# Attention and a gated MLP in one kernel: tokens walked from last to first, weights loaded over 128 partitions, and new orders from a changed plan

## The chip, the core and the metric

The kernel runs on one core of one Trainium2 chip. The metric is the device time of one execution in microseconds (us); the time of before is the median of three runs. A profile of one further execution, with its trace, is read for the reasons.

## The reference, cut to what matters

The input is x, 2048 tokens of 448 features, in bfloat16. The first half is attention in 16 heads of 28, in which a token sees 8 tokens at distances 0, 2, ..., 14 before it. The second half is an MLP whose gate mixes all tokens by a 2048x2048 matrix.

```
def _A_ref(x, wqkv, wo):            # W, dil = 8, 2
    q, k, v = (x @ wqkv) in 16 heads of 28
    idx = pos[:, None] - arange(W) * dil      # mask idx < 0
    logits = einsum('bhsd,bhswd->bhsw', q, k[idx]) * scale
    o = einsum('bhsw,bhswd->bhsd', softmax(logits), v[idx])
    return o @ wo
def _B_ref(x, w_in, w_sp, b_sp, w_out):
    z = gelu(x @ w_in)                        # 1792 columns
    z1, z2 = z[..., :896], layernorm(z[..., 896:])
    g = einsum('ts,bsf->btf', w_sp, z2) + b_sp[None, :, None]
    return (z1 * g) @ w_out
h = x + _A_ref(layernorm(x), A_wqkv, A_wo)
h2 = h + _B_ref(layernorm(h), B_w_in, B_w_sp, B_b_sp, B_w_out)
```

## The kernel before, in words

**Layout.** The 2048 tokens are 16 blocks of 128; block u and block u+8 make unit u (8 units), since the two halves of the sequence are worked on side by side. The 448 features are 7 chunks (NC7) of 64, so that two matmuls with 64 rows each run beside each other on TensorE: the first half of the tokens on partitions 0 to 63, the second half on 64 to 127 (index s in the loops). So each weight has to stand twice, on both halves of the partitions. Before, it is loaded from memory to partitions 0 to 63 (`ld_w` L546, `ld_win` L556, seven rows of 64 partitions), and VectorE (DVE) or ScalarE (ACT) copies it to the other half (`t_cp` L748, `cpw` L569). For q and k the copies also spread the heads from 28 to 32 columns. The weights of q and k are staged in z2p; those of v go straight to reg1 (reg1, reg2 and reg3 are memory that holds different things one after the other).

**The stages.** `ln_unit` (L633) normalizes a unit: statistics of two blocks on DVE (L639, L640), the reciprocal root on GpSimd (L629, L630) or ACT (L651, L652), the normalization on DVE into a ring tile tring (L659), and a transpose into xh, either on TensorE (L675, with a copy out of PSUM, L624 or L626) or by a transposing DMA (L666). For the first layernorm, `DMA_T` says which units go by DMA: 3 to 7. Then come the products for q and k (L787, in four column ranges CQ and CK of 128, 128 or 142, 256 and 512 tokens), nine attention tiles of 114 tokens (values L825, logits L859, exp L871, band mask L878, sums L887, weighted values L907, ln and exp for the division L895 and L917, the division L925), the output product L960 with the residual L968, the second layernorm, z2 (L980) and z1 (L1024), the big token mixing (L1060), its gate (L1069, L1077), and the last product (L1089), whose eviction with the residual (L1099) goes to tring and from there to memory (L1104). Names in the plan: x7 is the load of block 7, mmq3_0 a q product of column range 3, mmv8 the values of tile 8, tD1_4 the transposing DMA of unit 4 in the first layernorm, wsp0_8 and wsp1_8 the transposing loads of block 8 of the mixing matrix (two halves), bb the bias load.

**The halo.** The second half of the sequence begins at token 1024 and needs the 14 tokens ahead of it. Before, these are loaded again (xhalo, L576), normalized apart (L693 to L718: statistics, root, L700, seven small transposes L708, a copy L715) and put into the columns ahead of xh; the k product then runs over 1038 columns instead of 1024.

**What sets the order.** `Sched.issue` (L99) records instructions with their semaphore waits. `SEQ` (L34) holds for each of five queues (SP, POOL, DVE, ACT, PE) the tasks in the order in which they are issued; `Planner.replay` (L289) walks these lists with modelled durations, and its result decides only which PSUM banks and ring slots a task takes. An engine works off its list in order: a task that waits holds up all behind it. Loads are issued by SP and ACT (SPq and ACTq in the trace). Loads of blocks of units 2 to 7 wait until block 8 has landed (L585).

**Fillers.** f0 (15 matmuls on a constant tile, L618), f1 and f2 (3 each) keep TensorE busy while the first units are normalized.

Of the kernel before, what the change touches and what calls it, by code (L numbers as in the profile page):

```python
# [6 lines left out]
D = 448  # L7
DH = 28
FH = 896
# [14 lines left out]
DMA_T = {1: range(3, 8), 2: range(8)}  # L24
# [196 lines left out]
class Planner:  # L221
# [21 lines left out]
    CHUNK, ASK, NEED = 256, 118, 434  # L243
    FETCH = (0.95, 2.5)

    def fetch(self, nmm, now, dur, commit=False):

        n, m = self.pe_n, 2 * nmm
        ka, kn, free, av, shift = self.k_ask, self.k_need, self.f_free, self.avail, 0.0
        new = []  # L250
        while True:
            a, b = self.CHUNK * ka + self.ASK, self.CHUNK * kn + self.NEED
            if min(a, b) > n + m:
                break
            if a < b:
# [33 lines left out]
    def replay(self, t0=0.7):  # L289
# [13 lines left out]
        for _ in tasks:  # L303
# [26 lines left out]
            if e == "pe":  # L330
                if t.nmm:
                    dur += self.fetch(t.nmm, now, dur, True)
# [830 lines left out]
```

## Time and profile before

| | |
|---|---|
| median of 3 runs | 248.61 us (247.55 to 248.67) |
| the profiled execution | 246.46 us, of which the span is 244.4 us |
| PE (TensorE) busy | 234.2 us, 96% of the span |
| DVE, ACT, GpSimd busy | 142.3, 88.8, 26.9 us |

The span is the time from the first to the last instruction that the profiler saw; 2.06 us of the profiled execution lie around it. Rows of the timeline give start, duration, engine, line, operation, the tiles written and read, the shape and the count, and in brackets how long the engine had stood idle before and what ended that. "issue" there means that nothing the profile shows was waited for. PEld is the loading of weights into TensorE, which overlaps the matmuls.

### The profile page before, as it was taken

How to read it: one execution, taken by the hardware profiler on the slowest of the kernel's cores; microseconds unless marked ns; L12 is line 12 of the kernel's file. 1: busy time of each engine (PE TensorE's matmuls, PEld its weight loads, DVE VectorE, ACT ScalarE, POOL GpSimd, SP SyncE). 2: the span in 40 equal slices, each digit the busy share in tenths (PEclk: the TensorE clock that was granted, in tenths of full speed). 3: DMA queues.
4: the chain of work that ended last, by engine and by line, in shares of the span. 5: the costliest groups of instructions: out<-in, count | busy, mean ns of one | idle time of the engine just before them, and what ended most of it. 6: DMA issues, size and time to landing. Idle time of an engine off the chain costs nothing.

```text
span 244.4 us, 6704 instructions
## 1 busy us (share of the span) xinstructions
PE 234.2 (96%) x3021; PEld 120.7 (49%) x3032; DVE 142.3 (58%) x283; ACT 88.8 (36%) x104; POOL 26.9 (11%) x67
## 2 busy tenths in 40 slices
PE   6878998999999999999999999999999999999995
PEld 2675863455555454544444444444444444444443
DVE  7995984969999799887900013244011417541844
ACT  2886967188978857765730000000000000000000
POOL 5051300000330050137200000000000000000000
PEclk9999999999999999999999999999999999999999
DMA  6964394793669955665545443200000000010113
GB/s 149 276 117 96 75 134 74 100 159 70 89 69 120 165 160 103 107 133 105 118 91 155 88 86 86 46 0 0 0 0 3 0 0 0 21 38 18 56 58 113
DMA packets 54580, 20.02 MB, mean 82 GB/s; under 512 B 46856, under 2 KB 54424, under 8 KB 54552
## 3 DMA queue, kind: packets, MB, share of 16 engines
q1 hardware_dynamic: 52728, 18.05, 38.7%
q10 hardware_dynamic: 1824, 1.55, 3.1%
q8 instruction: 23, 0.38, 0.7%
q14 instruction: 5, 0.04, 0.1%
HBM read 6.39 MB, written 1.84 MB: 34 GB/s over the span
## 4 chain that ended last, share of the span: by engine, by line
PE 83%; DMA 9%; DVE 4%; issue 2%; SPq 1%; ACT 0%; DVEq 0%
PE psum L1060 39%; PE psum L980 9%; PE psum L1024 9%; PE psum L1089 9%; DMA wspT_lo<-in_B_w_sp_dram 6%; PE psum L787 5%; PE psum L960 4%; PE psum L825 4%; PE psum L859 1%; DMA xh<-tring 1%; PE psum L907 1%; DVE st L639 1%; DMA reg<-in_A_wo_dram 1%; PE psum L675 1%; DVE tring L659 1%
## 5 line engine op out<-in xcount | busy, mean ns | idle before, releaser
L1069 DVE TENSOR_TENSOR ub<-psum,reg 128x512 bf16<-128x512 f32 x28 | 18.8, 687 | 67.4 <-PE psum L1060 67.3
L1060 PE MATMUL psum<-reg,z2p 128*128 128x512 bf16 x219 | 49.4, 379 | 0.3
L1060 PE MATMUL psum<-wspT_lo,z2p 128*128 128x512 bf16 x218 | 48.5, 379 | 0.4 <-issue 0.2
L1060 PEld LDWEIGHTS psum<-wspT_lo,z2p 128*128 128x128 bf16 x224 | 21.8, 98 | 26.6 <-issue 0.4
L1060 PEld LDWEIGHTS psum<-reg,z2p 128*128 128x128 bf16 x224 | 21.9, 98 | 26.1
L787 PE MATMUL psum<-xh,reg 64*128 64x128 bf16 (+3 forms) x448 | 26.1, 270 | 1.2 <-issue 1.1
L980 PE MATMUL psum<-w_in,xh 64*128 64x448 bf16 x224 | 22.4, 349 | 0.1
L1089 PE MATMUL psum<-reg 128*128 128x448 bf16 (+1 forms) x119 | 22.3, 341 | 0.0
L1024 PE MATMUL psum<-xh,w_in 64*128 64x512 bf16 x196 | 22.0, 376 | 0.0
L787 PEld LDWEIGHTS psum<-xh,reg 64*128 64x128 bf16 x448 | 17.1, 94 | 9.0 <-issue 2.1
L624 ACT ACTIVATE reg<-psum 128x896 bf16<-128x896 f32 (+3 forms) x23 | 19.0, 843 | 3.6 <-PE psum L825 2.5
L639 DVE BATCH_NORM_STATS2 st<-x_tm 128x6 f32<-128x448 bf16 x32 | 19.5, 608 | 0.1
L996 DVE BATCH_NORM_STATS2 st<-z2p 128x6 f32<-128x448 bf16 x32 | 17.6, 607 | 2.4 <-ACT z2p L990 2.4
L871 ACT ACTIVATE reg<-psum 128x928 bf16<-128x928 f32 x18 | 16.2, 940 | 5.4 <-PE psum L859 5.4
L1099 DVE TENSOR_TENSOR tring<-psum,x_tm 128x448 bf16<-128x448 f32 (+1 forms) x17 | 9.8, 593 | 14.3 <-PE psum L1089 14.2
L1034 ACT ACTIVATE reg<-psum 128x1024 bf16<-128x1024 f32 x14 | 13.7, 1030 | 9.3 <-PE psum L1024 9.3
L1089 PEld LDWEIGHTS psum<-reg 128*128 128x128 bf16 x119 | 11.6, 98 | 10.2
L990 ACT ACTIVATE z2p<-psum 128x896 bf16<-128x896 f32 x16 | 14.1, 921 | 5.3 <-PE psum L980 5.2
L980 PEld LDWEIGHTS psum<-w_in,xh 64*128 64x128 bf16 x224 | 10.7, 94 | 10.7 <-issue 0.4
L630 POOL TENSOR_TENSOR rs<-rs,nhalf 128x2 f32<-128x2 f32 x20 | 15.5, 777 | 1.7
L1024 PEld LDWEIGHTS psum<-xh,w_in 64*128 64x128 bf16 x196 | 9.5, 94 | 11.4 <-ACT reg L1034 0.2
L629 POOL TENSOR_SCALAR rs<-mv 128x2 f32<-128x2 f32 x20 | 5.3, 263 | 87.7 <-DVE mv L640 77.4
(66 smaller groups left out, 201.7 us busy)
## 6 DMA issues: line engine op xcount, KB each, us to landing
out_dram<-tring SPq DMA_DIRECT2D x15, 112.0 KB, 1.7
x_tm<-in_A_x_dram SPq DMA_DIRECT2D x13, 112.0 KB, 4.6
w_in<-in_B_w_in_dram SPq DMA_DIRECT2D x2, 448.0 KB, 5.4
z2p<-in_A_wqkv_dram ACTq DMA_DIRECT2D x2, 392.0 KB, 6.0
reg<-in_B_w_out_dram SPq DMA_DIRECT2D x1, 784.0 KB, 4.8
w_in<-in_B_w_in_dram SPq DMA_DIRECT2D x2, 336.0 KB, 5.1
reg<-in_B_b_sp_dram SPq DMA_DIRECT2D x1, 512.0 KB, 3.7
reg<-in_A_wo_dram SPq DMA_DIRECT2D x4, 98.0 KB
```

The costliest lines, as they stand in the source:

```text
L624: iss("act", lambda e: e.activation(dst, src, AF.Copy), reads=rd, writes=wr)
L630: iss("pool", lambda e: e.tensor_tensor(dst, dst, nh, ALU.pow), reads=rr + [r_nhalf], writes=rr)
L639: iss("dve", lambda e: e.bn_stats(st[:, b, :], x_tm[:, b, :]), reads=[r_x[b]], writes=[rl[b]])
L787: iss("pe", lambda e, c=c, s=s, gi=gi, lhs=lhs: e.matmul(psum[:, bk[s] * 512 + cw * gi:bk[s] * 512 + cw * gi + cw], lhs, xh[64 * s:64 * s ...
L871: iss("act", lambda e: e.activation(E[:, es[0], 2 * n:2 * n + 2, :], pair_view(lb, 0, 8 * JW), AF.Exp, scale=SCALE), reads=[r_bank[lb[0]], ...
L980: iss("pe", lambda e, c=c, s=s: e.matmul(psum[:, zb[s] * 512:zb[s] * 512 + D], xh[64 * s:64 * s + 64, c, HX + 128 * u:HX + 128 * u + 128], ...
L990: iss("act", lambda e: e.activation(z2p[:, u:u + 9:8, D * k:D * k + D], pair_view(zb, 0, D), AF.Gelu_apprx_tanh), reads=[r_bank[zb[0]], r_ ...
L996: iss("dve", lambda e, b=b: e.bn_stats(st3[:, b, k, :], z2p[:, b, D * k:D * k + D]), reads=[r_z2[b][k]], writes=[r_st3[b][k]])
L1024: iss("pe", lambda e, c=c, s=s: e.matmul(psum[:, bk[s] * 512:bk[s] * 512 + 512], w_in[64 * s:64 * s + 64, c, 128 * f:128 * f + 128], xh[64 ...
L1060: iss("pe", lambda e, b=b: e.matmul(psum[:, gb[0] * 512:gb[0] * 512 + 512], z2p[:, b, 128 * f:128 * f + 128], src[:, b, 512 * (tc % 2):512 ...
L1069: iss("dve", lambda e: e.tensor_tensor(ub[:, us_[0], :], psum[:, gb[0] * 512:gb[0] * 512 + 512], bb[:, 512 * tc:512 * tc + 512], ALU.add), ...
L1089: iss("pe", lambda e, f=f: e.matmul(psum[:, wb[0] * 512 + d0:wb[0] * 512 + d1], z1p[f][:, 128 * m:128 * m + 128], w_out[:, f, d0:d1], star ...
```

## The change

Parts that belong together:

1. Units and attention tiles run from last to first. Unit 7 (blocks 7 and 15) comes first, tile 8 is the first tile; `S_ORDER` runs backward too, so that the mixing starts with blocks 7 and 15.
2. The halo is a copy: the 14 columns are copied on DVE from unit 7's xh on the other half of the partitions (`xpad`) for the values, and in kT (`kh`) for the keys. The load, the statistics and the seven small transposes go; the k product has 1024 columns. An attention tile's queries are shifted by 2 columns, and the mask with them.
3. Weights are loaded as 128-partition pieces: 384 rows as 3 x 128, the last 64 rows apart. Block m of the piece then holds chunk 2m on the lower and chunk 2m+1 on the upper half. Copies go crosswise between the halves (`cross`, and 16 copies instead of 8 for q and k), and `BLK` gives the order in which a half meets its chunks.
4. The plan's model of TensorE's instruction fetch counts a fetch into the queue of the loads (`resolve`); all lists in SEQ are new. The six pieces of wqkv and four x loads may go by SP or by ACT (`both`).
5. In the new lists f1 and f2 stand behind all other work of PE, and five of the last products (blocks 1, 6, 7, 0, 11) behind the split one of block 15.

```diff
-DMA_T = {1: range(3, 8), 2: range(8)}
+DMA_T = {1: range(5), 2: range(8)}
+BLK = ((0, 2, 4, 6, 1, 3, 5), (1, 3, 5, 0, 2, 4, 6))
...
+    def resolve(self, until, n=0):
+
+        while len(self.avail) < len(self.asks):
+            en = max([self.asks[len(self.avail)]] + self.avail[-1:]) + self.FETCH[0]
+            if en > until and len(self.avail) >= n:
+                break
+            st = max(en, self.qfree)
+            self.qfree = st + self.OCC
+            self.avail.append(st + self.FETCH[1])
...
+        def w_view(dst, src):
+            return ((dst[:, 0:3, :], src[0:384].rearrange("(m p) n -> p m n", p=128), 302.0),
+                    (dst[0:64, 3, :], src[384:448], 178.0))
...
-            t_w[p] = dma(eng, "w" + p, lambda e: e.dma_start(
-                w_st[p], A_wqkv[:, c0:c0 + D].rearrange("(c p) n -> p c n", p=64)),
-                D * D * 2, writes=[r_st[p]], bw=172.0)
+            for n, (dst, src, bw) in enumerate(w_view(w_st[p], A_wqkv[:, c0:c0 + D])):
+                t_w[p].append(dma(eng, "w%s%d" % (p, n), lambda e, dst=dst, src=src: e.dma_start(dst, src),
+                                  (384, 64)[n] * D * 2, writes=[r_st[p][n]], bw=bw, both=True))
+        def cross(name, w, rs, deps, n):
...
+            for h, lo, nb in ((0, 4, 3), (1, 3, 4)):
...
+                    copy(tk[0].eng, w[64 * h:64 * h + 64, lo:NC7, :], w[64 - 64 * h:128 - 64 * h, 0:nb, :], rs[:-2], [rs[h - 2]])
...
-        t_xhalo = dma("sp", "xhalo", lambda e: e.dma_start(xhalo[:, :], X[ST - 16:ST, :]), 16 * D * 2, writes=[r_xhalo])
...
+        t_xpad = cst("xpad", [(lambda e: e.tensor_copy(xh[64:128, :, HX - HALO:HX], xh[0:64, :, HX + ST - HALO:HX + ST]),
+                               [r_xh[NU - 1]], [r_xpad[1]])], 0.2, eng="dve", deps=[t_xh[NU - 1]])
...
-        CQ = [0, 128, 256, 512, ST]
-        CK = [0, 128, 270, 526, ST + HALO]
+        CQ = [0, 512, 768, 896, ST]
+        CK = [HALO + c for c in CQ]
...
+        t_kh = cst("kh", [(lambda e: e.tensor_copy(kT[:, 1, :, 0:HALO], kT[:, 0, :, ST:ST + HALO]), r_k[NCH - 1], [r_kh])], 0.15,
+                   eng="dve", deps=t_k[NCH - 1] + [c_kpad])
...
+        t_cp["v", 0] = cross("cpv", wv, r_w["v"], t_w["v"], D)
...
-        S_ORDER = [b for u in range(NU) for b in (u, u + 8)]
+        S_ORDER = [b for u in range(NU - 1, -1, -1) for b in (u, u + 8)]
...
+            t_hT[u] = ln_unit(u, 2, [th, th], [t_xpad] if u == NU - 1 else [])
```

The beginning of ACT's list, before, where the first loads are issued (x_tm blocks, then the weights of k and q into z2p, later v into reg1):

```order
L541 DMA x_tm<-in_A_x_dram 128x448 x3
L548 DMA z2p<-in_A_wqkv_dram 64x7x448 x2
L498 ACT_TABLE_LOAD
L651 ACTIVATE rs<-mv,epst 128x2
L652 ACTIVATE rs<-rs 128x2
L651 ACTIVATE rs<-mv,epst 128x2
L652 ACTIVATE rs<-rs 128x2
L624 ACTIVATE reg<-z2p 64x7x8x28
L624 ACTIVATE xh<-psum 128x7x128
L624 ACTIVATE reg<-z2p 64x7x8x28
L548 DMA reg<-in_A_wqkv_dram 64x7x448
```

The same stretch of ACT's list in the changed kernel (block 7, then q in two pieces, the small piece of v, the big piece of k):

```order
L539 DMA x_tm<-in_A_x_dram 128x448
L552 DMA z2p<-in_A_wqkv_dram 128x3x448
L552 DMA z2p<-in_A_wqkv_dram 64x448
L552 DMA reg<-in_A_wqkv_dram 64x448
L552 DMA z2p<-in_A_wqkv_dram 128x3x448
L494 ACT_TABLE_LOAD
L654 ACTIVATE rs<-mv,epst 128x2
L655 ACTIVATE rs<-rs 128x2
L627 ACTIVATE reg<-z2p 64x3x8x28
L654 ACTIVATE rs<-mv,epst 128x2
L655 ACTIVATE rs<-rs 128x2
L627 ACTIVATE reg<-z2p 64x4x8x28
```

Two of the three x loads have left ACT's queue, q stands ahead of k, and a piece of every weight is issued ahead of the table load. The other pieces are in SP's list, which begins with x14, x15, x6, the big piece of v, x13, x9, x12, the small piece of k, x4, x2 and two pieces of w_in.

The beginning of PE's list, before, and then in the changed kernel:

```order
L618 MATMUL psum<-warm 128x512 x15
L675 MATMUL psum<-ident,tring 128x128 x7
L618 MATMUL psum<-warm 128x512 x3
L675 MATMUL psum<-ident,tring 128x128 x7
L618 MATMUL psum<-warm 128x512 x3
L708 MATMUL psum<-ident,thalo 128x16 x7
L787 MATMUL psum<-xh,reg 128x142 x56
L787 MATMUL psum<-xh,reg 128x128 x168
L859 MATMUL psum<-reg 64x58 x64
L825 MATMUL psum<-reg,xh 64x448 x56
```

```order
L621 MATMUL psum<-warm 128x512 x15
L678 MATMUL psum<-ident,tring 128x128 x14
L769 MATMUL psum<-xh,reg 128x128 x28
L809 MATMUL psum<-reg,xh 64x448 x56
L769 MATMUL psum<-xh,reg 128x128 x196
L678 MATMUL psum<-ident,tring 128x128 x7
L844 MATMUL psum<-reg 64x58 x96
L769 MATMUL psum<-xh,reg 128x256 x112
```

The fillers between the transposes and the halo's transposes are gone, the first product of q is followed by the values of tiles 8 and 7, and all 224 matmuls of the first two column ranges have 128 columns.

The end of PE's list, before, and then in the changed kernel:

```order
L1060 MATMUL psum<-reg,z2p 128x512 x16
L1089 MATMUL psum<-reg 128x448 x14
L1060 MATMUL psum<-reg,z2p 128x512 x16
L1089 MATMUL psum<-reg 128x448 x21
L1089 MATMUL psum<-reg 128x224 x14
```

```order
L1050 MATMUL psum<-reg,z2p 128x512 x16
L1079 MATMUL psum<-reg 128x448 x21
L1079 MATMUL psum<-reg 128x224 x14
L1079 MATMUL psum<-reg 128x448 x35
L621 MATMUL psum<-warm 128x512 x6
```

Five products of full width now follow the two of half width, and the six filler matmuls come last.

More of the change, by code (lines that the diff above doesn't have):

```diff
@@ L243, with fetch @@
     CHUNK, ASK, NEED = 256, 118, 434
[L244 to L250, printed above, removed]
+    FETCH, OCC, DMA_LAT = (1.09, 2.55), 0.72, 1.15
+    def resolve(self, until, n=0):
[6 more added lines that the diff above has]
+            self.avail.append(st + self.FETCH[1])
+    def fetch(self, nmm, now, dur):
+        n, m, shift = self.pe_n, 2 * nmm, 0.0
         while True:
-            a, b = self.CHUNK * ka + self.ASK, self.CHUNK * kn + self.NEED
+            a, b = self.CHUNK * len(self.asks) + self.ASK, self.CHUNK * self.k_need + self.NEED
             if min(a, b) > n + m:
@@ L331, in replay @@
                 if t.nmm:
-                    dur += self.fetch(t.nmm, now, dur, True)
+                    dur += self.fetch(t.nmm, now, dur)
                 if t.mode != pe_mode:
@@ L518, in dve4x, with dma @@
             return (190.0 + 0.26 * n) / 1000.0
-        def dma(eng, name, fn, nbytes, deps=(), reads=(), writes=(), rel=(), store=False, issue=0.62, bw=288.0, after=(), setup=1.45):
+        def dma(eng, name, fn, nbytes, deps=(), reads=(), writes=(), rel=(), store=False, issue=0.62, bw=302.0, after=(), setup=1.35, both=False):
             def em():
@@ L535, in dma @@
             t.setup = setup
+            if both:
+                t.alts = {"sp": issue, "act": issue}
             return t
@@ L577, in bass_sequential_preLN__sliding_local_dilated__mixer_gmlp__prompt_kernel @@
+            t_win[z] = tl + cross("cpw%d_" % z, w, r_win[z], tl, FH)
+        ld_x(7)
+        ld_x(15, "act")
+        ld_w("k", "act")
+        ld_x(6, "sp")
+        ld_x(14, "sp")
         ld_w("q", "act")
-        ld_x(1, "act")
-        ld_x(9, "act")
-        ld_w("k", "act")
         ld_w("v", "act")
-        for u in range(2, NU):
+        for u in range(5, -1, -1):
             ld_x(u)
             ld_x(u + 8)
-        for u in range(2, NU):
+        for u in range(6):
             for b in (u, u + 8):
-                t_x[b].deps.append(t_x[8])
-                t_x[b].waits.append(t_x[8])
+                t_x[b].deps += [t_x[7], t_x[15]]
+                t_x[b].waits += [t_x[7], t_x[15]]
@@ L768, in bass_sequential_preLN__sliding_local_dilated__mixer_gmlp__prompt_kernel @@
         qk_all = []
-        for ch in range(NCH):
+        for ch in range(NCH - 1, -1, -1):
             for isq in (0, 1):
-                t0, t1 = (CQ if isq else CK)[ch:ch + 2]
+                t0, t1 = CQ[ch:ch + 2]
                 cw = t1 - t0
-                off = HX if isq else HX - HALO
-                us = units(t0, t1) if isq else units(t0 - HALO, t1 - HALO)
+                off = 2 if isq else HALO
+                us = units(t0, t1)
                 per = 2 if cw <= 256 else 1
@@ L779, in bass_sequential_preLN__sliding_local_dilated__mixer_gmlp__prompt_kernel, with em @@
                     bk = []
-                    rx = [r_xh[b] for b in us] + ([r_xpad] if (t0 == 0 and not isq) else [])
-                    def em(t0=t0, cw=cw, isq=isq, g0=g0, bk=bk, ng=ng, off=off, p=p, rx=rx):
+                    rx = [r_xh[b] for b in us]
+                    def em(t0=t0, cw=cw, g0=g0, bk=bk, ng=ng, p=p, rx=rx):
                         for gi in range(ng):
@@ L943, in ld_wsp @@
                 dst[:, b, :], B_w_sp[1024 * half:1024 * half + 1024, 128 * b:128 * b + 128], transpose=True),
-                128 * 1024 * 2, deps=deps, writes=[r_wsp[b][half]], after=extra, issue=1.25, bw=129.0, setup=0.64)
-        S_ORDER = [b for u in range(NU) for b in (u, u + 8)]
+                128 * 1024 * 2, deps=deps, writes=[r_wsp[b][half]], after=extra, issue=1.25, bw=125.0, setup=0.25)
+        S_ORDER = [b for u in range(NU - 1, -1, -1) for b in (u, u + 8)]
         for n, b in enumerate(S_ORDER):
             ld_wsp(b, 0)
-        t_h = []
-        t_hT = []
+        t_h = [None] * NU
+        t_hT = [None] * NU
         t_z2 = [None] * NB
-        for u in range(NU):
+        for u in range(NU - 1, -1, -1):
             bk = []
@@ L1113, in chain @@
                 t.waits.append(d)
-        for n, t in enumerate(ld_in):
-            t.deps += [t_xh[3 + n], ld_in[n - 1] if n else None]
-            t.deps = [d for d in t.deps if d is not None]
-        chain([t_wsp[b][0] for b in S_ORDER], t_xh[NU - 1])
+        chain([t_wsp[b][0] for b in S_ORDER], t_xh[0])
         chain([t_wsp[b][1] for b in S_ORDER], t_wout)
```

250 lines of the change are left out of this document (106 added, 144 removed), and 62 rows, old and new, of the table SEQ.

## The prediction

> **What bounds the kernel now.** The first part of the page says which engine fills the span; the chain of waits says what the end hangs on.
>
> ```profile
> PE 234.2 (96%) x3021; PEld 120.7 (49%) x3032; DVE 142.3 (58%) x283; ACT 88.8 (36%) x104; POOL 26.9 (11%) x67
> PE 83%; DMA 9%; DVE 4%; issue 2%; SPq 1%; ACT 0%; DVEq 0%
> ```
>
> TensorE (PE) is the bound, so what can be gained is what PE does not spend on products: the time ahead of the first product, holes, and the time behind the last matmul. The timeline of PE and the end of the chain, in order of time, give all three:
>
> ```profile
> 10.01 5.66 PE L787 MATMUL psum<-xh,reg 64*128 64x142 bf16 x180
> 16.79 1.40 PE L787 MATMUL psum<-xh,reg 64*128 64x128 bf16 x44 [1.13 <-issue]
> 20.90 2.05 PE L825 MATMUL psum<-reg,xh 64*64 64x448 bf16 x37 [0.90 <-issue]
> 38.91 0.70 PE L859 MATMUL psum<-reg 32*64 32x58 bf16 x61 [1.21 <-issue]
> 236.27 5.23 PE psum L1089 x34
> 241.52 0.06 DVE tring L1099
> ```
>
> The first product starts at 10.01 us; the last matmul ends at 241.5, and 2.9 us of eviction and store follow. Of the holes between, the waits of PE show that none of size is a wait for data:
>
> ```profile
> PE psum L859 <- issue: 1.4, 2, 1.2
> PE psum L787 <- issue: 1.1, 1, 1.1
> PE psum L825 <- issue: 0.9, 1, 0.9
> PE psum L907 <- issue: 0.2, 1, 0.2
> PE psum L1060 <- issue: 0.2, 1, 0.2
> ```
>
> Together 3.8 us. They come at regular counts: from the hole at 16.79 (222 matmuls into PE's list) to that at 20.90 (350) are 128 matmuls, each with its weight load, so 256 instructions; the hole at 38.9 stands four such steps on (about 860). So PE is waiting for its own instructions. Their queue carries 23 packets of 0.38 MB, 16 KB each, and asking the DMA view in short windows finds them: none from 0 to 14 us, then one each in 14.0 to 14.5, 18 to 19 and 36 to 37 us:
>
> ```profile
> q8 instruction: 23, 0.38, 0.7%
> q8 instruction: 1, 0.02, 17.2%
> q8 instruction: 1, 0.02, 8.5%
> q8 instruction: 1, 0.02, 6.9%
> ```
>
> PE resumes some 2.7 us after each packet. The first came only when the loads had drained. The table by stages shows that (last column GB/s, the one before it the share of DMA time):
>
> ```profile
> 2.00:4.00 2.00, 2.00 (x5) 0.70 (x6) 1.92 (x4) 0.40 (x1) 1.13 (x5) 1.00 0.99 231
> 4.00:6.00 2.00, 2.00 (x9) 0.82 (x8) 1.90 (x7) 1.13 (x2) 1.32 (x5) 1.00 0.88 203
> 6.00:9.00 3.00, 2.68 (x23) 1.37 (x22) 2.91 (x9) 2.38 (x6) 0.00 (x0) 1.00 1.14 192
> 9.00:12.00 3.00, 2.68 (x75) 2.23 (x75) 2.90 (x7) 2.81 (x3) 0.00 (x0) 1.00 1.10 355
> 12.00:14.30 2.30, 2.18 (x80) 2.04 (x76) 2.16 (x7) 2.29 (x4) 1.21 (x3) 1.00 1.12 224
> 14.30:17.00 2.70, 1.57 (x58) 1.40 (x53) 2.60 (x6) 2.24 (x6) 2.25 (x8) 1.00 0.05 8
> ```
>
> The engines are full from 2 to 14.3 us, but move 192 and 224 GB/s while 64-partition weights are among the loads, and 355 where x (128 partitions) runs nearly alone. From one late fetch to the next lie 4.1 us (16.79 to 20.90) although the queue was empty at first: the next fetch is asked for only when the last has arrived. I read a late fetch as queue plus 2.7 us, and 4.1 us as its shortest cycle.
>
> [...]
>
> **The head.** What leads to 10.01 us:
>
> ```profile
> 3.47 0.58 DVE L639 BATCH_NORM_STATS2 st<-x_tm 128x6 f32<-128x448 bf16 x1
> 5.64 0.59 DVE L639 BATCH_NORM_STATS2 st<-x_tm 128x6 f32<-128x448 bf16 x1
> 6.37 1.08 DVE L659 TENSOR_SCALAR tring<-x_tm,mv,rs 128x448 bf16<-128x448 bf16 x3
> 7.38 1.51 ACT L624 ACTIVATE reg<-z2p 64x1568 bf16<-64x1568 bf16 x1 [0.36 <-DMA z2p<-in_A_wqkv_dram]
> 8.80 0.89 ACT L624 ACTIVATE xh<-psum 128x896 bf16<-128x896 bf16 x1
> 9.75 0.33 PE L708 MATMUL psum<-ident,thalo 16*128 16x16 bf16 x7 [0.32 <-ACT xh L624]
> 10.78 0.61 DVE L626 COPY reg<-z2p 64x1568 bf16<-64x1568 bf16 x1
> 15.63 0.97 DVE L626 COPY reg<-reg 64x3136 bf16<-64x3136 bf16 x1
> x_tm<-in_A_x_dram ACTq DMA_DIRECT2D x3, 112.0 KB, 2.5
> ```
>
> Behind the halo's statistics DVE starts x at 3.47 and takes 0.72 per block (three steps to 5.64). ACT waits for k's weights, copies 1.51, evicts xh until 9.69, and the halo's transposes close the head. In the new order DVE starts as x14 lands: 2.5 us from an issue at 0.8, so 3.3 at the latest; I take 3.1. Four blocks to 6.0; four normalizations of 0.36 (1.08 for three) are 1.4; between them two q copies. The two copy rows give 0.25 plus 0.23 ns per element, so 0.46 for 64x896 and 0.40 for 64x672, 0.9 together; a copy of xh of 0.6. That is 8.9 us: **-1.1**. It holds if q is there by 6.0. Ahead of its last byte stand, both queues sharing, four x blocks (0.46 MB), q (0.40) and half of what SP has put behind (0.17): 1.03 MB from 2.0 us. At 271 GB/s or more it is in time; at the 217 of the first two rows it lands at 6.75 plus some 0.3, 0.7 late, and the head gains 0.4. With no wait anywhere it gains 1.4.
>
> **The fetch holes.** PE's next need for instructions comes, as before, near matmul 217 of its list. From the first product to there now stand 132 matmuls of 128 columns at 31 ns (1.40 us for 44 in the 16.79 row, the last one's end taken off) and 56 of L825 at 52 (2.05 for 37 in the 20.90 row): 4.1 + 2.9 = 7.0 us, where before 180 took 5.66. So it comes at 8.9 + 7.0 = 15.9, and no hole arises if the packet passes by 13.2. Ahead of it then stand what SP and ACT have issued by about 11 us (SP issues a load per 0.45 to 0.65 us): 13 x blocks (1.49 MB), all of wqkv (1.20), three pieces of w_in (0.80) and one of wo (0.10), some 3.6 MB where before 3.05 had to drain. In 128-partition loads are 3.2 MB, at 355 GB/s 9.0 us; the narrow 0.39 MB at 205 take 1.9. That ends at 12.9: just in time. I take a hole of 0.3. The next 128 matmuls take about 3.65 us: 92 products of 31 ns, 29 logits of 11 (0.70 for 61 in the 38.91 row), and seven transposes, for which I take 0.5. That is less than the cycle of 4.1: 0.45. The third hole (matmul 860) meets transposing loads in both kernels; but the plan's constants put the request 158 matmuls ahead of the need, and in that stretch now stand more products of 512 columns and fewer short matmuls; I take 0.5 for 1.21. The last small ones stay (0.5). Sum 1.75 instead of 3.8: **-2.05**, with bounds of 0 and 3.2, from holes that stay to nothing left of the large three.
>
> **The columns.** 56 matmuls lose 14 of their columns; at 31 ns for 128, 0.24 each, that is 56 x 14 x 0.24 ns = **-0.2**.
>
> **The tail.** The last matmuls now feed a full eviction and store instead of half ones:
>
> ```profile
> L1099 DVE TENSOR_TENSOR tring<-psum,x_tm x17: 381/623/625, 205.8 to 241.8; 128x448 bf16<-128x448 f32 x15, 128x224 bf16<-128x224 f32 x2
> out_dram<-tring SPq DMA_DIRECT2D x15, 112.0 KB, 1.7
> out_dram<-tring SPq DMA_DIRECT2D x2, 56.0 KB, 1.6
> ```
>
> 0.62 - 0.38 + 0.1 = **+0.35**. The six fillers behind them run while the store does: at the 0.4 of the slow fillers below 2.4 us, less than the 2.9, and nothing waits for PE.
>
> **What I cost at nothing.** The eight more weight copies are 8 x 0.25 us over DVE and ACT between 6 and 18 us; PE's products from 8.9 on cover them, but ACT's evictions stand behind its copies. From 5.3 it has two roots of 0.5, six copies of 6048 elements at 0.96 ns (1.51 us for 1568) and xh at 0.89 ahead of the first eviction, which so starts at 13.0; PE wants that PSUM pair back at some 13.5 (8.9, with two L825 groups and two products of q between). Without cover this costs up to 0.5, within my range. The two halo copies (98 columns, 0.2 each) lie where DVE is a follower. The new wait: tD2_7 on SP waits for `xpad`, and behind it wait wsp0 loads and the first z2 product; h7 is now the first residual of its stage, several tiles ahead of that product. In the mixing the bias is issued behind 13 transposing loads instead of 9:
>
> ```profile
> 131.47 0.58 SPq L1042 DMA_DIRECT2D reg<-in_B_b_sp_dram  x1
> 136.39 17.51 SPq L942 DMA_TRANSPOSE reg<-in_B_w_sp_dram  x6
> 123.74 11.60 PE L1060 MATMUL psum<-wspT_lo,z2p 128*128 128x512 bf16 x52 [0.16 <-issue]
> ```
>
> At 2.9 us per load that is up to 12 us later, less what the chain starts earlier (it no longer stands behind as many wsp0 loads). PE fills its eight banks with 112 matmuls of 0.22, until 148; only then would it wait for the bias. I expect it near 140; landing at 150 would cost 2.
>
> **Sum.** -1.1 - 2.05 - 0.2 + 0.35 = -3.0 us. Against the profiled execution (246.46: 244.4 of span, 2.06 around it) that is 243.5. The median of the runs stands 2.15 higher, at 248.61, and I shift by the same: **245.6 us**. Its own range, by the bounds of head (-0.4 to -1.4) and holes (-1.0 to -3.2), is 244.0 to 247.4.
>
> **Rivals.** (1) The holes do not shrink: the fetch takes its cycle of 4.1 us whatever the loads do, or a hole at one place moves to another. For it speaks that the 20.90 hole stood in an empty queue; against it that the first packet passed just as the loads ended. -1.1 - 0.2 + 0.35 = -0.95: 247.7.
>
> (2) The clock. The weight loads of f0's first seven matmuls came some 0.4 us apart, the last seven took 1.39 us, 0.2 each, though the granted clock stands at 1.00 in all rows:
>
> ```profile
> 4.50 0.15 PEld L618 LDWEIGHTS psum<-warm 128*128 128x128 bf16 x1 [0.28 <-issue]
> 4.89 1.39 PEld L618 LDWEIGHTS psum<-warm 128*128 128x128 bf16 x7 [0.24 <-issue]
> ```
>
> Without f1 and f2 only 14 transposes lie between f0's end, near 6.4, and the first product at 8.9. If PE falls back to half pace, it needs the first time's 2.9 us again (from the filler's start near 2.0 to 4.89) and loses half of them, 1.5: 247.1. Against it: the hole of 1.13 us left L787 at 32 ns per matmul. [...]
>
> (3) Slower: the longer load queue. If it drains at the 224 GB/s of the 12.0 row, 3.6 MB end at 18.1 and PE resumes at 20.8. The head then gains 0.4 only, the need comes at 16.6, and the hole is 4.2 us. With 0.45, 1.2 and 0.5 for the others that is 6.35 instead of 3.8: +2.55 - 0.4 - 0.2 + 0.35 = +2.3, so 250.9. It decides from about 260 GB/s downward. For it: that is the mean of before (3.05 MB in 12.3 us, 248). Against it: 355 where loads are wide.
>
> **Chances and range.** Forecast 0.60, holes stay 0.17, clock 0.08, longer queue 0.15. A measurement of this kernel can tell about 0.5% from no change, 1.2 us. Faster by more: 0.58 of the forecast, 0.04 of the clock, 0.03 of the staying holes, 0.65; within 0.5%: 0.20; slower: 0.15. The range reaches from the forecast's fast end over rivals 1 and 2: 244.0 to 248.8.
>
> **What would show it.** First L769 product near 8.9; a q8 packet by about 13 us; GB/s above 320 from 3 to 12 us; PE's waits marked issue below 2 us in all; the last matmul 3.2 to 3.5 us ahead of the end. Wrong it would be by new waits of PE for ACT or DVE between 13 and 80 us, which no row of before shows, or by the bias.

## The result and the profile after

| | before | after |
|---|---|---|
| median, first comparison (4 runs each) | 248.08 us (246.99 to 248.67) | 244.06 us (243.78 to 244.94) |
| ratio, 95% interval | | 0.9849 (0.9802 to 0.9896) |
| ratio in a second comparison with more runs | | 0.9873 (0.9822 to 0.9923) |
| profiled execution (span) | 246.46 us (244.4) | 243.78 us (242.0) |

Faster by 1.3 to 1.5%, so 3 to 4 us by the medians and 2.7 us by the two profiled executions. The ratios are those of the fast runs: in the second comparison three of after's seven runs (247.2 to 247.7 us) and one of before's eleven (250.1) do not enter, and with them the means are 245.3 and 247.0 us. The forecast was 245.6, the range 244.0 to 248.8. First, PE's timeline of the kernel after: start, duration, engine and line, shape, count, and in brackets how long PE had stood idle and for what. L769 is the product of q and k (L787 before), L678 the transposes of the head, L950 and L897 the matmuls of a later stage.

```profile
8.75 0.56 PE L678 MATMUL psum<-ident,tring 128*128 128x128 bf16 x7 [0.85 <-DVE tring L662]
9.29 0.95 PE L769 MATMUL psum<-xh,reg 64*128 64x128 bf16 x28
...
14.24 4.89 PE L769 MATMUL psum<-xh,reg 64*128 64x128 bf16 x168 [0.25 <-ACT reg L627]
...
32.54 3.20 PE L769 MATMUL psum<-xh,reg 64*128 64x512 bf16 x28 [1.24 <-DMA xh<-tring]
...
64.54 0.36 PE L950 MATMUL psum<-reg 128*128 128x448 bf16 x1 [0.76 <-issue]
...
68.91 0.20 PE L897 MATMUL psum<-reg 64*32 64x58 bf16 x2 [0.32 <-issue]
```

Products start at 9.29 instead of 10.01. All three large holes marked issue (16.8, 20.9, 38.9 us) are gone: 168 products run through without a break where the first stood. One large wait is new, 1.24 us for a transposed block (and a small one, 0.25 for ACT), and small fetch holes are left behind 60 us. The waits of PE marked issue in sum (total, times, longest):

```profile
PE psum L950 <- issue: 0.8, 1, 0.8
PE psum L897 <- issue: 0.3, 1, 0.3
```

So fetch takes 1.1 us where it took 3.8. The stage table, in the same windows as before (last column GB/s), says why:

```profile
2.00:4.00 2.00, 2.00 (x6) 0.67 (x5) 1.11 (x3) 0.43 (x1) 1.51 (x8) 1.00 0.95 282
4.00:6.00 2.00, 2.00 (x6) 0.76 (x5) 1.93 (x6) 1.25 (x3) 0.00 (x0) 1.00 1.09 355
6.00:9.00 3.00, 2.15 (x17) 1.05 (x16) 2.73 (x9) 2.91 (x6) 0.00 (x0) 1.00 1.13 330
9.00:12.00 3.00, 2.98 (x72) 2.30 (x73) 2.85 (x8) 2.98 (x4) 0.26 (x1) 1.00 1.01 358
12.00:14.30 2.30, 2.05 (x54) 1.39 (x48) 2.22 (x7) 2.28 (x4) 1.33 (x6) 1.00 0.87 241
```

Between 4 and 9 us the engines now move 330 to 355 GB/s where they moved 192 to 203. The DMA view in windows of 0.1 us puts the first instruction packet at 12.8 us (14.0 before) and the next at 16.8, 21.1 and 25.3. In the window from 12.5 to 13.0 us, which holds the first:

```profile
q8 instruction: 1, 0.02, 15.2%
```

The new data wait is followed back along three queues: DVE's mask and normalizations, POOL's root and SP's transposing load of unit 3 (blocks 3 and 11; called block 3 below), each with its start and duration.

```profile
25.45 1.12 DVE L863 TENSOR_TENSOR reg<-reg,mband 128x1856 bf16<-128x1856 bf16 x1
27.16 0.70 DVE L662 TENSOR_SCALAR tring<-x_tm,mv,rs 128x448 bf16<-128x448 bf16 x2 [0.60 <-POOL rs L633]
25.70 1.43 POOL L633 TENSOR_TENSOR rs<-rs,nhalf 128x2 f32<-128x2 f32 x1
27.89 1.22 SPq L669 DMA_TRANSPOSE xh<-tring  x1
```

With the order turned round, units 0 to 3 come last. Their four transposing loads stand in a row on SP, the last is issued at 27.89 us, as soon as its normalization ends (27.86), and PE wants it at 31.3.

### The profile page after: what moved, and what is told of

Read it like the earlier page. It is cut to its first block, busy times and chain, and to the rows that moved or that the text cites. A ratio compares the mean times of both kernels' runs of the same rounds, so it can differ in the third digit from the quotient of the medians.

```text
span 242.0 us, 6725 instructions
## 1 busy us (share of the span) xinstructions
PE 235.2 (97%) x3025; PEld 121.2 (50%) x3025; DVE 139.2 (58%) x283; ACT 93.1 (38%) x108; POOL 26.9 (11%) x70
## 4 chain that ended last, share of the span: by engine, by line
PE 84%; DVE 8%; DMA 3%; ACT 2%; issue 1%; POOL 1%
PE psum L1050 40%; PE psum L970 9%; PE psum L1079 9%; PE psum L1014 9%; PE psum L769 5%; PE psum L950 5%; DVE st L642 3%; PE psum L809 3%; PE psum L844 2%; DMA xh<-tring 2%; DVE tring L662 2%; PE psum L897 2%; DVE reg L629 2%; DVE mv L643 1%; DMA x_tm<-in_A_x_dram 1%
## 5 line engine op out<-in xcount | busy, mean ns | idle before, releaser
L1050 PE MATMUL psum<-wspT_lo,z2p 128*128 128x512 bf16 x224 | 49.0, 379 | 0.0
L769 PE MATMUL psum<-xh,reg 64*128 64x128 bf16 (+2 forms) x448 | 25.9, 270 | 1.6 <-DMA xh<-tring 1.2
L970 PE MATMUL psum<-w_in,xh 64*128 64x448 bf16 x224 | 22.4, 349 | 0.0
L627 ACT ACTIVATE reg<-psum 128x1024 bf16<-128x1024 f32 (+2 forms) x25 | 20.4, 863 | 3.7 <-PE psum L769 3.5
L769 PEld LDWEIGHTS psum<-xh,reg 64*128 64x128 bf16 x448 | 16.9, 94 | 9.2 <-ACT reg L885 1.3
L633 POOL TENSOR_TENSOR rs<-rs,nhalf 128x2 f32<-128x2 f32 x21 | 16.5, 784 | 1.7
L970 PEld LDWEIGHTS psum<-w_in,xh 64*128 64x128 bf16 x224 | 10.5, 94 | 10.8 <-issue 0.8
```

Of the source, the lines that this page charges most:

```text
L627: iss("act", lambda e: e.activation(dst, src, AF.Copy), reads=rd, writes=wr)
L633: iss("pool", lambda e: e.tensor_tensor(dst, dst, nh, ALU.pow), reads=rr + [r_nhalf], writes=rr)
L769: iss("pe", lambda e, c=c, s=s, gi=gi, lhs=lhs: e.matmul(psum[:, bk[s] * 512 + cw * gi:bk[s] * 512 + cw * gi + cw], lhs, xh[64 * s:64 * s ...
L970: iss("pe", lambda e, k2=k2, c=BLK[s][k2], s=s: e.matmul(psum[:, zb[s] * 512:zb[s] * 512 + D], xh[64 * s:64 * s + 64, c, HX + 128 * u:HX + ...
L1050: iss("pe", lambda e, b=b: e.matmul(psum[:, gb[0] * 512:gb[0] * 512 + 512], z2p[:, b, 128 * f:128 * f + 128], src[:, b, 512 * (tc % 2):512 ...
```

## The experiments

In the short diffs the lists are written with the names of tasks instead of their numbers (x14 is the load of block 14, tD1_3 the transposing load of block 3, cpq a copy of q's weights, mml logits, mmq a product of q, mmo a tile's second product, rs a root).

### Before, with late loads moved back

```diff
-SP: xhalo x0 x4 x3 x5 x11 x13 x7 x2 x10 x12 x6 wo1 x15 tD1_3 x14 win1_0 ...
+SP: xhalo x0 x3 x5 x11 x13 x2 x10 x15 tD1_3 x14 x7 x4 x6 x12 wo1 win1_0 ...
```

> The kernel before, with five loads that nothing needs early (x blocks 4, 6, 7 and 12 and one piece of wo, 0.56 MB) moved in SP's list behind block 14 of x and a transposing load; every other row as before. Theory (PE's holes marked issue are instruction packets that stand behind the queued loads): the first packet passes near 12 us instead of 14.0 to 14.5, the holes at 16.8 (1.13 us) and 20.9 (0.90) shrink to below 0.3 together, the hole near 39 stays or moves, so about -1.7 us. Rival (the fetch takes its own cycle whatever the loads do): the same two holes at the same matmul counts, and the time within 0.5 us of before.

Ratio to before 0.9965 (0.9935 to 0.9994). PE's timeline of this kernel (L799 is L787 of before, L837 is L825, L919 is L907):

```profile
10.53 6.93 PE L799 MATMUL psum<-xh,reg 64*128 64x142 bf16 x224
...
20.18 2.05 PE L837 MATMUL psum<-reg,xh 64*64 64x448 bf16 x37 [1.01 <-issue]
...
24.84 6.17 PE L799 MATMUL psum<-xh,reg 64*128 64x256 bf16 x109 [0.80 <-issue]
30.94 0.68 PE L919 MATMUL psum<-reg 64*32 64x58 bf16 x64
```

The packet came at 13.2 us instead of 14.0, and the hole at 16.8 is gone: 224 products in one row where before broke off after 180. (PE's first product also starts 0.52 us later here, for reasons in the head, and that alone would have made the hole smaller by as much; the packet does the rest.) So a packet does stand behind the loads that are queued ahead of it. But the next packets came at 17.8 and 21.7, and PE met holes of 1.01 and 0.80, the first at the matmul count of before's second hole. At the matmul that starts at 30.94 here, before is at 30.84: by then nothing is left of the gain: the hole that was taken out at one packet came back at the next. The theory was right on the cause of the first hole and wrong on the size (-0.9 us by the ratio instead of -1.7). The trace does not show where even that comes from: this execution took 247.38 us, more than before's 246.46, with waits of 0.59 for ACT and 0.71 for a transposed block behind 55 us.

### After, with 1 MB more in the load queue

```diff
-SP: ... x11 x10 x1 wo1 win1_2 ...
+SP: ... x11 x10 x1 dum0 dum1 wo1 win1_2 ...
+            dma("sp", "dum%d" % n, lambda e, n=n: e.dma_start(
+                wspT_lo[:, 2 * n:2 * n + 2, :].rearrange("p b t -> p (b t)"), B_w_sp[128 * n:128 * n + 128, :]), ...)
```

> The kernel after, with two more loads of 0.5 MB each (rows of w_sp, into a buffer that the transposing loads fill later) in SP's list behind block 1 of x. They do work that the reference does not ask for. Theory (the instruction packet stands behind the queued loads): 1.05 MB more at 355 GB/s is 2.9 us, the first packet comes at 14.5 to 15.5 us instead of 12 to 13, a hole marked issue of 1.5 to 2.5 us opens before matmul 217 of PE's list, near 16 us, and the time rises by 1.5 to 3 us. Rival (the packets do not depend on the loads): no such hole, and less than +0.6 us.

Ratio to before 1.0031 (0.9994 to 1.0069), so about 1.6 to 1.8% above after, some 4 us; span 244.8 instead of 242.0. PE's timeline:

```profile
17.54 2.63 PE L783 MATMUL psum<-xh,reg 64*128 64x128 bf16 x88 [0.65 <-issue]
...
22.77 0.71 PE L858 MATMUL psum<-reg 32*64 32x58 bf16 x65 [1.74 <-issue]
```

The packets passed at 14.9 and 20.4 us, and PE resumed 2.6 and 2.3 us behind them. The theory holds: more in the load queue, a later packet, a hole. The first hole is smaller than expected (0.65 for 1.5 to 2.5), the larger one came at the next packet, 5.5 us behind the first, and the time rose by more than the 1.5 to 3 us expected.

### After, with narrow loads

```diff
-                    (dst[:, 0:3, :], src[0:384].rearrange("(m p) n -> p m n", p=128), 302.0),
+            half = src[0:384].rearrange("(m h p) n -> h p m n", h=2, p=64)
+                    (dst[0:64, 0:3, :], half[0], 172.0), (dst[64:128, 0:3, :], half[1], 172.0),
(the 128-partition pieces of w_in in the same way)
```

> The kernel after, with each 128-partition weight load of wqkv and w_in split into two loads of 64 partitions into the same places; the same bytes, five or so more issues on each queue. Theory (64-partition loads drain at about 200 GB/s, 128-partition ones at about 355): the stages from 2 to 12 us fall to 200 to 250 GB/s, the head ends 0.3 to 1 us later, the first packet passes at 15 us or later with a hole of 1.5 to 3 us near matmul 217, time +2 to +4 us. Rival (the width of the loads does not matter, the gain of the change came from order and head alone): GB/s as after, within 0.6 us of after.

Ratio to before 1.0062 (1.0025 to 1.0099): with narrow loads the whole change is slower than no change, and about 2% (4.6 to 5.2 us) above after. The stage table and PE's timeline of this kernel:

```profile
4.00:6.00 2.00, 2.00 (x6) 0.76 (x5) 1.93 (x6) 0.72 (x1) 0.00 (x0) 1.00 0.90 267
6.00:9.00 3.00, 2.08 (x12) 0.80 (x10) 1.84 (x7) 2.79 (x7) 0.00 (x0) 1.00 1.13 256
9.00:12.00 3.00, 2.17 (x51) 1.76 (x55) 2.91 (x8) 2.98 (x4) 0.00 (x0) 1.00 1.11 259
```

```profile
10.34 0.96 PE L786 MATMUL psum<-xh,reg 64*128 64x128 bf16 x28
...
18.36 2.67 PE L786 MATMUL psum<-xh,reg 64*128 64x128 bf16 x89 [0.62 <-issue]
...
22.78 0.74 PE L861 MATMUL psum<-reg 32*64 32x58 bf16 x65 [0.88 <-issue]
```

The same bytes now drain at 256 to 267 GB/s instead of 330 to 358, with a DMA share of 0.90 to 1.13 (1.01 to 1.13 in after). The head ends 1.05 us later, the packet passes at 15.5, and the holes are back. (Splitting also adds issues on the queues; how much of the 5 us is theirs was not tried apart. And the trace holds a wait of 1.79 us for a transposed block near 85 us, which after's second profile, with wide loads, shows too: see below.) Why narrow loads drain more slowly no row shows.

### After, with the root of block 3 on ACT

```diff
-POOL: ... rs1_2 rs1_3 rs2_7 ...      ACT: ... evq1_0 evq1_2 ...
+POOL: ... rs1_2 rs2_7 ...            ACT: ... evq1_0 rs1_3 evq1_2 ...
```

> The kernel after, with the one root of the normalization of block 3 moved from POOL (where it took 1.4 us after another root) to ACT, behind an eviction of q. Theory (the new wait of 1.24 us at 31.3 us for the transposed block 3 hangs on that root, its normalization and one transposing load): the load is issued 0.6 to 1 us earlier, the wait falls to 0.3 to 0.7, time -0.5 to -0.9 us. Rival (the wait hangs on the transposing loads ahead of it in SP's queue, or ACT's later eviction takes the gain back): the wait stays at 1 us or more or a wait for ACT of the same size appears, time within 0.3 us of after.

Ratio to before 0.9923 (0.9894 to 0.9952), so no better than after. Its rows of DVE, SP and PE for the same block:

```profile
26.46 0.69 DVE L676 TENSOR_SCALAR tring<-x_tm,mv,rs 128x448 bf16<-128x448 bf16 x2
28.43 1.30 SPq L683 DMA_TRANSPOSE xh<-tring  x1
33.76 4.88 PE L783 MATMUL psum<-xh,reg 64*128 64x512 bf16 x28 [1.99 <-DMA xh<-tring]
```

The normalization runs 0.7 us earlier, the transposing load is issued 0.5 us later. The one ahead of it held SP for 2.62 us instead of 1.64, so the rival is right: here the wait hangs on SP's transposing loads. In five other executions of kernels with this order the same wait was 1.24, 0, 1.62, 1.18 and 0.94 us.

### After, with independent work in the gap

```diff
-PE:  ... mmo8_3 mmq0_1 mmq0_0 mmo7_0..3 mml5_00..11 mmq0_3 ...    ACT: ... rex8 rex7 evq0_0 exp5_0 evq0_3 exp5_1 ...
+PE:  ... mmo8_3 mml5_00..11 mmq0_1 mmo7_0..3 mmq0_0 mmq0_3 ...    ACT: ... rex8 exp5_0 exp5_1 rex7 evq0_0 evq0_3 ...
```

> The kernel after, with tile 5's logits (four groups of 16 short matmuls, 0.7 us) moved on PE ahead of the products of q that wait for the transposed block 3, tile 7's second product between these, and the two exponentials of tile 5 ahead of two other rows on ACT. Theory (the wait of 1.2 us is only a gap in PE's order and independent work can stand in it): the wait falls to 0.4 to 0.8, no new wait for ACT or DVE behind it, span -0.6 us against after. Rival (the banks that the logits hold make the later products wait for ACT): a wait of 0.5 us or more marked ACT or DVE between 32 and 40 us, span the same.

Ratio to before 0.9878 (0.9829 to 0.9927), the same as after in the same comparison (0.9873). The rows of PE around the gap (in this execution the granted clock fell to 0.5 at 63 us, so the rows behind 60 us say nothing on the gap):

```profile
31.87 0.25 PE L858 MATMUL psum<-reg 32*64 32x58 bf16 x6 [0.20 <-ACT reg L899]
32.38 0.41 PE L858 MATMUL psum<-reg 32*64 32x58 bf16 x26 [0.26 <-issue]
```

The wait for the transposed block is gone, 0.46 us of small waits stand in its place, and no larger one follows before 60 us. But since the wait it fills varies between 0 and 2 us by itself, the worth of this in the time stays open.

### After, once more; and before, a second profile

> The kernel after once more, with more runs beside the kernel before on one chip, since before's runs lie from 244.6 to 248.4 us and four of them carried the first ratio. By the two traces (span 244.4 and 242.0) the change is worth -2.4 us, ratio 0.990; by the first medians -4.0, ratio 0.985. The traces' theory: 0.989 to 0.992, with before's runs spread by holes that fall differently in each run. Rival: 0.985 or less, and something in most of before's runs that its profiled execution did not show. Its profile should again show the wait of 1 to 2 us for the transposed block 3 and no hole marked issue of over 0.4 us before 60 us.

> The kernel before, a second profiled execution. Theory (fetch holes): the three holes marked issue stand again at the same counts of matmuls (222, 350 and some 860), 2.5 to 3 us behind a packet each, with sizes that differ by up to 0.5 us from the first profile. Rival (the holes were an accident of that execution): they stand elsewhere or are absent.

The second ratio, 0.9873 (0.9822 to 0.9923), lies between the two expectations, and its interval holds both the 0.989 of the traces and the 0.985 of the first runs. Before's profile has the three holes again, at the same counts of products, with packets in the half microseconds from 14.0, 18.0 and 36.0 us:

```profile
17.19 1.40 PE L787 MATMUL psum<-xh,reg 64*128 64x128 bf16 x44 [1.55 <-issue]
...
20.75 2.05 PE L825 MATMUL psum<-reg,xh 64*64 64x448 bf16 x37 [0.45 <-issue]
...
38.49 0.70 PE L859 MATMUL psum<-reg 32*64 32x58 bf16 x61 [0.94 <-issue]
```

The places are fixed by the instruction count; the sizes vary by 0.3 to 0.5 us. A longer first hole (1.55 for 1.13) made the second shorter (0.45 for 0.90): the packets set the pace, not the holes. In after's second profile the first hole of over 0.4 us came at 61 us, and the wait for block 3 was not there at all, against what was expected of it.

That execution took 247.15 us, and its trace shows why. Up to 60 us it is level with the first profile. Then come a hole, a stretch in which the granted clock is 0.50 (the column ahead of the last two), and a wait in the second layernorm's stage (L970 is the product z2):

```profile
61.71 0.42 PE L844 MATMUL psum<-reg 32*64 32x58 bf16 x25 [0.67 <-issue]
64.00:64.50 0.50, 0.50 (x3) 0.24 (x2) 0.45 (x2) 0.50 (x2) 0.00 (x0) 0.50 0.32 6
84.71 5.47 PE L970 MATMUL psum<-w_in,xh 64*128 64x448 bf16 x56 [1.95 <-DMA xh<-tring]
80.19 3.29 SPq L669 DMA_TRANSPOSE xh<-tring  x2
```

At 79.56 us PE starts work that the first profile starts at 78.12, so hole and clock cost 1.4 us, and the wait adds 1.95. SP issued the two transposing loads at 80.19 where the first profile issued the first of them at 74.29: the w_sp loads ahead of them in SP's list were issued every 4.5 us instead of 3.5, each waiting for an earlier one to land (in after SP waited 11 times for that on the first half of w_sp, 20.6 us in all). The profiles of the kernels with narrow loads (1.79) and with independent work in the gap (1.89) show the same wait. Why the w_sp loads land more slowly in these executions is open.

### After, with block 15 last

```diff
-PE: ... wo14_0_6 wo15_0_0 wo15_1_0 wo15_0_6 wo15_1_6 wo1_0_0 wo6_0_0 wo7_0_0 wo0_0_0 wo11_0_0 f1 f2
+PE: ... wo14_0_6 wo1_0_0 wo6_0_0 wo7_0_0 wo0_0_0 wo11_0_0 wo15_0_0 wo15_1_0 wo15_0_6 wo15_1_6 f1 f2
(DVE's additions and SP's stores in the same order)
```

> The kernel after, with block 15's output last again, in two halves, as in the kernel before. The prediction's term (a full eviction and a full store at the end cost 0.35 more than half ones): the last matmul stands 2.4 to 2.5 us ahead of the end instead of 2.79. The theory from before's trace (both halves are evicted behind the last matmul, 0.69 us together, and only the store is smaller): 2.8 to 2.9 us.

The last eviction and the end of the last product in after, and then in this kernel (rows of the timeline and of the chain):

```profile
239.25 0.62 DVE L1089 TENSOR_TENSOR tring<-psum,x_tm 128x448 bf16<-128x448 f32 x1 [0.70 <-PE psum L1079]
227.27 11.94 PE psum L1079 x70
```

```profile
238.70 0.69 DVE L1103 TENSOR_TENSOR tring<-psum,x_tm 128x224 bf16<-128x224 f32 x2 [0.62 <-PE psum L1093]
226.82 11.94 PE psum L1093 x70
```

From the end of the products to the end of the span: 242.0 - 239.21 = 2.79 us in after, 241.6 - 238.76 = 2.84 here (2.88 in before). The prediction's 0.35 us does not exist (this kernel's one run took 243.35 us, 0.4 less than after's profiled execution, which is within the spread of after's runs). Two halves evicted one behind the other take 0.69, a full block 0.62.

### After, with two of the head's copies on POOL

```diff
-DVE:  ... nrm1_7 cpq000 nrm1_15 nrm1_6 cpq011 nrm1_14 ...   ACT: ... rs1_7 cpq001 rs1_6 ...
+DVE:  ... nrm1_7 nrm1_15 nrm1_6 nrm1_14 ...                 ACT: ... rs1_7 rs1_6 cpq001 ...
+POOL: ... c_wkp cpq000 cpq011 rs1_4 ...
```

> The kernel after, with the two copies of q's weights that DVE makes between its normalizations (0.38 and 0.39 us) given to POOL, which has nothing to do from 3.9 to 11.7 us, and ACT's root for block 6 one place earlier. Theory (what leads to the first product is DVE's row of statistics, copies and normalizations): DVE's last normalization of the head ends 0.6 to 0.8 us earlier, the wait of 0.85 before the second seven transposes falls below 0.4, the first product starts at 8.6 to 8.9 instead of 9.29, time -0.4 to -0.7 us. Rival (POOL's copies are slow, or slow down DVE beside them): POOL takes over 1 us per copy, the first product waits for POOL at 9.3 us or later, time the same or up to +1.

Ratio to before 0.9957 (0.9919 to 0.9995). POOL's copies, the first product, and DVE's four normalizations of the head as a group (count, busy, mean ns); behind it the same group in after:

```profile
6.38 1.79 POOL L643 COPY reg<-z2p 64x896 bf16<-64x896 bf16 x2 [2.45 <-DMA z2p<-in_A_wqkv_dram]
9.28 0.96 PE L783 MATMUL psum<-xh,reg 64*128 64x128 bf16 x28
L676 DVE TENSOR_SCALAR tring<-x_tm,mv,rs 128x448 bf16<-128x448 bf16 x4 | 2.4, 658 | 0.0
```

```profile
L662 DVE TENSOR_SCALAR tring<-x_tm,mv,rs 128x448 bf16<-128x448 bf16 x4 | 1.5, 386 | 0.2 <-ACT rs L655 0.2
```

The rival is right, in its second form: DVE is rid of 0.77 us of copies, and its normalizations beside POOL's copies take 0.27 us longer each (658 ns for 386), so that the first product starts at 9.28, as in after (9.29). Why they take longer no row shows.

### After, with the fillers back in the head

```diff
-PE: f0 tT1_7 tT1_6 mmq3_0 ... wo11_0_0 f1 f2
+PE: f0 tT1_7 f1 tT1_6 f2 mmq3_0 ... wo11_0_0
```

> The kernel after, with the two fillers f1 and f2 of three 512-column matmuls back between the transposes of the head and ahead of the first product. Theory (the first product waits for DVE and ACT, and the clock holds without the fillers): the first product starts at 9.3 to 10.0, 0 to 0.7 us later, all granted clocks 1.00 in both, the 28 first products take 0.95 us in both. Rival (the head without fillers leaves PE slower): the first 28 products and the 56 behind them take less time than the 0.95 and 2.84 us of the kernel after.

```profile
10.14 0.95 PE L783 MATMUL psum<-xh,reg 64*128 64x128 bf16 x28
11.03 2.85 PE L823 MATMUL psum<-reg,xh 64*64 64x448 bf16 x56
```

The first product starts 0.85 us later, directly behind f2, and the first 28 and 56 matmuls take just as long as in after (0.95 and 2.84). So the head without fillers costs PE no pace, and leaving them out is worth most of a microsecond, more than the head gained in all. (Its single time, 249.06 us, holds a fetch hole of 2.52 us and a stretch of half clock behind 60 us and is no measure of the fillers.)

No version beat after by more than these runs can tell.

## Why the prediction came out as it did

**The bound and the reading of the holes: right.** That PE waited for instruction packets, and these for the loads, is shown by two kernels that change only the queue: with loads moved back the first packet is 0.8 us earlier and its hole gone; with 1 MB more it is 2.1 us later and a hole opens. The 2.7 us from packet to resumption held in all of them within 2.3 to 3.1. But 4.1 us is not the shortest cycle, as the prediction had it: in before itself packets pass at 22.4 and 25.9 us, 3.5 apart. When a fetch is asked for no run shows: that the next is asked for only when the last has arrived was the author's reading, and the 158 matmuls from request to need are a constant of the plan. In before the holes cost 3.8 us.

**The head: right in kind, 1.1 forecast, 0.72 measured.** The rows of DVE that were summed:

```profile
3.24 0.63 DVE L642 BATCH_NORM_STATS2 st<-x_tm 128x6 f32<-128x448 bf16 x1 [0.85 <-DMA x_tm<-in_A_x_dram]
6.31 0.36 DVE L662 TENSOR_SCALAR tring<-x_tm,mv,rs 128x448 bf16<-128x448 bf16 x1
8.61 0.62 DVE L629 COPY xh<-psum 128x896 bf16<-128x896 bf16 x1
```

x came 0.14 later than the 3.1 assumed, and the four blocks of statistics took 3.07 instead of 2.9; the rest (2.3 from the first normalization to the copy of xh, then 0.6) was as forecast. q's weights were in time. What the sum did not name: the fillers had to leave as well. With them in place the first product starts at 10.14, where before had it at 10.01, so shortening DVE's row alone would have gained nothing. In before they cost nothing, since PE waited 0.32 us for ACT behind them.

**The fetch holes: -2.05 forecast, -2.7 measured, and +1.5 not foreseen.** The three large ones went altogether. The second had been given 0.45, as what the cycle of 4.1 us leaves behind a first packet that is just in time, and the third 0.5. The packets did come every 4.0 to 4.3 us up to 25 us, but the first was early: 12.8 plus 2.7 is 15.5, and PE comes to matmul 217 of its list only at about 16.4 (counted along PE's timeline). The next 128 matmuls took about 3.4 us and used up some 0.6 of these 0.9 us; behind them the products of 256 columns (112 in 6.31 us) are slower than the packets. The small holes behind 60 us grew from 0.6 to 1.1. The term that was missing is the wait for data behind them: PE, earlier by the holes, met the transposed block 3 (1.24) and ACT's first eviction (0.25). The latter was in the text, with the eviction at 13.0 (13.59 in the trace) and a price of up to 0.5. The former was only named as what would be wrong, a new wait between 13 and 80 us, and named for ACT and DVE, not for the transposing loads, though the reversed order puts four of them in a row ahead of the first product that needs all of them.

**The columns: -0.2, not to be seen.** Of the 1.59 us that the stretch from first product to last matmul lost (231.51 to 229.92), fetch and the two new waits explain 1.2; of the other 0.4, 0.16 is a wait of before for wo that is gone, and the rest holds the columns and whatever else is of that size.

**The tail: +0.35 forecast, -0.1 measured.** The failing step is "a full eviction and store instead of half ones": the half ones stand one behind the other, which a row of before already said (two of 128x224 in one group behind the last matmul).

**What was costed at nothing: right in after's first profile, not in every execution.** The bias reached DVE at 141.8 (forecast near 140) and PE's chain shows no break there. The weight copies cost 0.25 us through ACT's eviction, as said above. The copy into xpad did hold up SP: it ended at 63.98 us, tD2_7 was issued at 64.01, and SP had been free for it since 61.1. PE felt nothing of it there. But the row of w_sp and transposing loads that stands behind tD2_7, and which the text names, made PE wait 1.8 to 2.0 us in three other profiles with the new order; in these SP came to tD2_7 late by itself, with the copy long done in after's second one (64.48, issued at 67.40).

**From the profile to the median: the step that missed most.** 243.5 was forecast for the profiled execution, and it took 243.78. Then 2.15 us were added because before's three runs lay that far above its profile. In later comparisons, on three chips, the medians of before were 246.28 (29 runs), 247.07 and 246.48 us, so its profiled execution (246.46) was an ordinary one and the three runs were high. After's runs lie at its profile (244.06 and 243.78). Hence the forecast of 245.6 came out 1.5 too high. Why the first runs of before were higher than the later ones (the draw, or the chip) is open.

**What was luck.** The difference of -3.0 us came close to the -2.7 of the profiled executions because errors cancel: the holes (0.65) and the tail (0.45) came out better than forecast, the head (0.4) and the waits (1.5) worse. And the measured 244.06 lies at the very edge of the range: the bounds as listed add up to 244.2 at the fast end, not to 244.0. The bound of 0 that the text gives for the holes became -1.0 in the range.

**The rivals.** Holes that stay: not in after, but the rival's second half, a hole that moves to another place, is what the kernel with late loads shows. The clock in the head: no, by the fillers' kernel. The longer load queue: it did not come, since the loads drained at 330 to 358 GB/s between 4 and 12 us. The same kernel with narrow loads drains at 256 to 267 and is slower than before by 0.25 to 1.0%, 1.5 us (0.6 to 2.5). That is near the point given for no gain, some 260 GB/s, and short of the 2.3 that the rival had for 224. In these lists the rest of the change would then not have paid: the wide loads decide the sign, as far as the added issues of the narrow ones leave it to them.

## What to carry to other kernels

In this kernel the holes marked issue at regular counts of matmuls were late instruction packets. Where such holes show, find the packets' times in the DMA view, look at what was queued ahead of the first, and remember that a gain at one packet is kept only if PE's next ones are not wanted faster than they come (in after they came every 4.0 to 4.3 us up to 25 us; with late loads the first hole, 1.13, went, and the next two were 1.01 and 0.80). Loads across all 128 partitions paid here even with blocks copied crosswise: they drained at 330 to 358 GB/s instead of 256 to 267, and the kernel with narrow loads, which also has more issues, took 4.6 to 5.2 us more. When an order is reversed, look for the inputs that now come last, and price their way to the engine that bounds; and do not move a forecast from the profile to the median by a draw of three runs.

## What the runs showed of the hardware

In three executions an idle time of PE of 0.67 to 1.99 us was followed by half of its clock. In the kernel with block 3's root on ACT the products behind the wait of 1.99 us took 4.88 us instead of 3.20; the windows (the column ahead of the last two is the granted clock) show it:

```profile
33.50:34.00 0.50, 0.24 (x4) 0.17 (x6) 0.00 (x0) 0.50 (x1) 0.00 (x0) 1.00 1.13 249
34.50:35.00 0.50, 0.50 (x6) 0.24 (x4) 0.00 (x0) 0.00 (x0) 0.00 (x0) 0.50 0.50 161
38.00:38.50 0.50, 0.50 (x6) 0.11 (x2) 0.50 (x1) 0.00 (x0) 0.00 (x0) 1.00 0.18 16
```

The clock is at 0.5 from about 34.3 to 37.7, some 3.4 us. In after's second profile a hole of 0.67 us came ahead of such a stretch (63.8 to 67.2), and 0.94 in the kernel with independent work in the gap. Yet 1.62 us at the place of block 3 in the kernel with block 15 last left the clock at 1.00, as did 1.55 us in before's second profile and 1.74 with 1 MB more. So the length of one idle time does not decide it; what does was not tried.

A POW of two columns on POOL (L633) took 1.43 us beside DVE's mask and 0.70 to 0.82 in 18 of the other 20 cases (0.97 and 1.15 in two near 115 us). With POOL's copies it was DVE that took longer (658 ns for 386); whether both have one cause was not tried.

The holes between 60 and 70 us vary most between executions: none in two of the kernels with the new order, 0.76 and 0.32 in after, 1.49 in the one with copies on POOL, 0.97 and 2.52 in the one with fillers. In after they too end 2.3 us behind a packet (62.2 and 66.6 us). The loads that SP issues then are transposing ones, nearly all of w_sp. What delays the packets there was not tried.
